# Three-layer attention and MoE chain in fp32 parts: the last two layers in token blocks of 512, 512, 512 and 256

## The chip, the cores and the metric

The kernel runs on one core of a Trainium2 chip. The metric is the device time of one execution in microseconds (us). The profile is of one execution of its own; its times are counted from the first instruction.

## What is computed

Attention with a sigmoid in place of the softmax (4 sequences, 12 heads, 448 tokens, head size 64), a layer that takes the maximum of three products and multiplies by an output matrix, and a layer with a gated unit of width 2048. All tensors are fp32.

```python
scores = q @ k.T / sqrt(64) - log(448)
x = (sigmoid(scores) @ v)                       # 1792 tokens x 768
h = maximum(maximum(x @ w1, x @ w2), x @ w3)    # layer one, 768 wide
y = h @ w_out                                   # layer two
h = y @ w_in                                    # layer three, 2048 wide
g = h * sigmoid(1.702 * h)
out = g @ w_out2                                # layer four
```

## The kernel before

TensorE multiplies in a type (fp32r) that keeps only the upper part of an fp32 number, so every operand is split into an upper and a lower part, and a product is three matmuls into the same PSUM bank: upper weights by upper data, upper weights by lower data, lower weights by upper data (lines 374 to 376, and 608 to 610). Weights are tiles of 128 by 128; the moving operand is 448 tokens wide, one sequence. Each matmul has its own weight load, also where two matmuls in a row use the same weights.

Stages. First, pairs of heads: scores (lines 424 and 426), sigmoid, and the product with the values (line 461, or line 453 in plain fp32 for six of the 24 pairs), in "beats" between which layers one and two of finished sequences are placed (`unit1`, `unit2`). Layer two writes its result, split in its parts (`yst`), to DRAM (`yk`, line 570), six tiles a sequence. Then layers three and four: the 2048 columns are taken in eight groups of two tiles of 128. For each group the four weight tiles are read and split (`weights2`), and for each of the four sequences `unit3` makes two tiles of layer three (6 input tiles x 3 matmuls each), passes each through a sigmoid (ScalarE), a product with it, and a split (VectorE, ScalarE), and `unit4` multiplies the two by the six output tiles (2 x 3 matmuls each) and adds each result to an accumulator in SBUF (`acc`, VectorE; in the first group a copy). `unit3` of the next block is written ahead of `unit4` of the present one. In the last group the accumulators go to DRAM; the last one is added and sent in two halves.

PSUM: layer three has two banks (`mms`), layer four six (`pos`). SBUF is allocated in two phases: the pools `late` and `acc` take over the space of the attention stage and of layers one and two when their last operation is done (`to_late`, `to_acc`). The inputs of layer three (`z`) are read back from DRAM once and stay; those of the first sequence (`z0s`) lie in `late`, the others (`zs`) in `acc`, so their reads wait for the end of layer two.

Order. All operations are first collected in an `Order`, with costs such as `MM` for a matmul and due times that follow from TensorE's order. `run` then lists them per engine by a simulated clock and writes the program out in that order; what an engine executes is fixed before the run, and each engine takes its instructions one after the other. A cast (`copy`) may go to ScalarE or VectorE, as the planner chooses.

Addresses. A weight tile begins at word 48 of its buffer (`OFF`), its data at word 0 (all sizes are multiples of 64 words). In the attention stage the keys, which are the weights there, begin at word 464 (`KEYS`), so 16 beyond a multiple of 64. The outputs of the gate, the moving operand of layer four, begin at the word given by `G_OFF` for their group: 0, 8, 16, 24, 32, 40, 4, 60.

## Time and profile before

| | us |
|---|---|
| median of 3 runs | 987.09 (986.69 to 987.25) |
| the profiled execution | 987.43 |
| its span, first to last instruction | 985.6 |
| TensorE busy in the span | 972.6 |
| VectorE busy | 621.8 |
| ScalarE busy | 347.5 |

Busy time of TensorE is a union of matmuls that overlap, so two matmuls that follow each other are told apart by their starts. PE in a row is TensorE's matmuls, PEld its weight loads, DVE is VectorE, ACT ScalarE, SP the queue that issues DMAs. A number after "L" is the line of the kernel; L225, L222 and L212 are the helpers `two` and `rest`, `copy` and `dma`, so there the tile names tell more.

### The profile page before, as it was taken

Reading aid. Unit: us, or ns where it says so; the run is one execution under the profiler, and the core shown is the slowest. Engines: PE = TensorE matmul, PEld = TensorE weight load, DVE = VectorE, ACT = ScalarE, POOL = GpSimd, SP = SyncE. Lnnn points to the kernel's source line nnn. Section 1 sums busy time; section 2 is a strip of 40 time slices with the busy share of each in tenths; the row PEclk is TensorE's granted clock in tenths of the full one; section 3 lists DMA queues with packets and bytes.
Section 4 is the critical chain, followed back from the end, with each engine's and each line's share of the span. In section 5 each row is a group of like instructions: output and inputs, shape, how many; then the busy total and the mean of one; then the engine's idle time right before and its main releaser. Section 6 shows DMA issues by size and latency. Waiting matters only on the chain.

```text
span 985.6 us, 12195 instructions
## 1 busy us (share of the span) xinstructions
PE 972.6 (99%) x4918; PEld 871.3 (88%) x4918; DVE 621.8 (63%) x945; ACT 347.5 (35%) x514; POOL 1.1 (0%) x6
## 2 busy tenths in 40 slices
PE   8899999999999999999999999999999999999998
PEld 5568888888888889999998999999999999999997
DVE  7989999997577747511112454776757576754344
ACT  6666666953454532111012441221222122121110
POOL 0000000000000000000000000000000000000000
PEclk9999999999999999999999999999999999999999
DMA  7856787996565659996668021110201111000023
GB/s 255 309 189 246 257 307 271 366 380 223 186 206 181 219 178 413 334 348 208 220 217 342 15 80 49 65 65 10 94 26 65 65 65 65 1 1 1 1 103 122
DMA packets 39656, 166.14 MB, mean 169 GB/s; under 512 B 4400, under 2 KB 10288, under 8 KB 39600
## 3 DMA queue, kind: packets, MB, share of 16 engines
q1 hardware_dynamic: 39600, 165.36, 46.7%
q8 instruction: 39, 0.64, 0.3%
q14 instruction: 17, 0.14, 0.0%
HBM read 129.96 MB, written 35.39 MB: 168 GB/s over the span
## 4 chain that ended last, share of the span: by engine, by line
PE 95%; DVE 2%; DMA 1%; issue 0%; SPq 0%; ACT 0%; DVEq 0%
PE mm L374 20%; PE mm L376 19%; PE mm L375 19%; PE po L608 8%; PE po L609 8%; PE po L610 8%; PE sc L424 4%; PE av L461 4%; PE av L453 3%; PE sc L426 1%; DMA raw<-in_wa 1%; PE av L465 1%; DMA v<-in_v 1%; DVE al L225 0%; DVE y L347 0%
## 5 line engine op out<-in xcount | busy, mean ns | idle before, releaser
L374 PE MATMUL mm<-x,w 128*128 128x448 f32 x432 | 159.5, 369 | 0.0
L376 PE MATMUL mm<-x,w 128*128 128x448 f32 x432 | 156.9, 363 | 0.0
L375 PE MATMUL mm<-x,w 128*128 128x448 f32 x432 | 156.6, 363 | 0.0
L225 DVE TENSOR_TENSOR acc<-po,acc 128x448 f32<-128x448 f32 (+1 forms) x169 | 103.8, 620 | 62.9 <-PE po L610 61.6
L608 PE MATMUL po<-g,w 128*128 128x448 f32 x384 | 140.2, 365 | 0.0
L374 PE MATMUL mm<-z,w 128*128 128x448 f32 x384 | 138.9, 362 | 1.2 <-DVE gf L225 1.2
L609 PE MATMUL po<-g,w 128*128 128x448 f32 x384 | 140.1, 365 | 0.0
L610 PE MATMUL po<-g,w 128*128 128x448 f32 x384 | 140.0, 365 | 0.0
L375 PE MATMUL mm<-z,w 128*128 128x448 f32 x384 | 139.4, 363 | 0.0
L376 PE MATMUL mm<-z,w 128*128 128x448 f32 x384 | 138.9, 362 | 0.0
L592 ACT ACTIVATE sg<-mm 128x448 f32<-128x448 f32 x64 | 34.9, 546 | 246.5 <-PE mm L376 246.5
L434 ACT ACTIVATE a<-sc,bias 128x896 f32<-128x896 f32 (+1 forms) x96 | 85.2, 915 | 54.4 <-PE sc L424 42.8
L225 DVE TENSOR_TENSOR gf<-mm,sg 128x448 f32<-128x448 f32 x64 | 39.9, 623 | 84.0 <-ACT sg L592 83.9
L374 PEld LDWEIGHTS mm<-x,w 128*128 128x128 f32 x432 | 80.9, 187 | 13.0 <-issue 7.3
L375 PEld LDWEIGHTS mm<-x,w 128*128 128x128 f32 x432 | 81.1, 188 | 6.3 <-issue 0.6
L376 PEld LDWEIGHTS mm<-x,w 128*128 128x128 f32 x432 | 81.1, 188 | 4.8
L225 DVE TENSOR_TENSOR mx<-mm,mx 128x448 f32<-128x448 f32 x48 | 30.0, 624 | 83.6 <-PE mm L376 83.2
L374 PEld LDWEIGHTS mm<-z,w 128*128 128x128 f32 x384 | 72.0, 187 | 7.0 <-issue 1.6
L610 PEld LDWEIGHTS po<-g,w 128*128 128x128 f32 x384 | 72.1, 188 | 5.8
L608 PEld LDWEIGHTS po<-g,w 128*128 128x128 f32 x384 | 72.0, 188 | 5.8
L609 PEld LDWEIGHTS po<-g,w 128*128 128x128 f32 x384 | 72.1, 188 | 5.7
L375 PEld LDWEIGHTS mm<-z,w 128*128 128x128 f32 x384 | 72.1, 188 | 5.1
(77 smaller groups left out, 1396.9 us busy)
## 6 DMA issues: line engine op xcount, KB each, us to landing
w<-kept SPq DMA_DIRECT2D x72, 768.0 KB, 5.0
raw<-in_wb SPq DMA_DIRECT2D x32, 768.0 KB, 5.3
raw<-in_wa SPq DMA_DIRECT2D x24, 768.0 KB, 4.4
kept<-w SPq DMA_DIRECT2D x24, 768.0 KB, 4.1
t<-in_qk SPq DMA_DIRECT2D x23, 488.0 KB, 4.3
yk<-yst SPq DMA_DIRECT2D x24, 448.0 KB, 5.5
z<-yk SPq DMA_DIRECT2D x24, 448.0 KB, 8.3
out_t<-acc SPq DMA_DIRECT2D x23, 224.0 KB, 1.9
```

The costliest lines, as they stand in the source:

```text
L225: return on("DVE", t_two(n), lambda: dve.tensor_tensor(to(), a(), b(), op=op), [a, b], [to])
L374: pe.matmul(ps(), wh[:, c], xh, start=k == 0, stop=False)
L375: pe.matmul(ps(), wh[:, c], lo(), start=False, stop=False)
L376: pe.matmul(ps(), wl[:, c], xh, start=False, stop=k == KC - 1)
L424: pe.matmul(o[:, e, :], kx[r, keys], qx[r, :S], **how)
L434: on("ACT", t_act(n) + 0.07, lambda: act.activation(a(), ps(), AF.Sigmoid, bias=bias, scale=scale), [ps], [a])
L453: pe.matmul(o, w, x[:, e, :] if c < 3 else x, start=c + e == 0, stop=c == 3)
L461: pe.matmul(av[e](), w, x()[:, e, :], start=c + n == 0, stop=False)
L592: on("ACT", t_act(S), lambda sg=sg, ps=ps: act.activation(sg(), ps(), AF.Sigmoid, scale=1.702), [ps], [sg])
L608: pe.matmul(ps(), wh[:, c], gh, start=j == 0, stop=False)
L609: pe.matmul(ps(), wh[:, c], gl, start=False, stop=False)
L610: pe.matmul(ps(), wl[:, c], gh, start=False, stop=j == 1)
```

## The change

Layers three and four take the 1792 tokens in blocks of 512, 512, 512 and 256 (`TB`) and no longer by sequence. `NB` is still four, so groups, units and their order stay.

For a block of 512 each product is three matmuls as before, with 512 columns. For the block of 256 the upper and lower part lie next to each other, and one matmul of 512 columns passes both through the upper weights: the first 256 columns of the bank get upper by upper, the others upper by lower. A second matmul of 256 columns adds lower weights by upper data to the first half (`terms`). The two halves are then summed: in layer three by a cast of the lower half and an addition ahead of the sigmoid, in layer four by two additions into the accumulator (in the first group a copy and an addition).

Layer two's tiles are cut where a block ends within a sequence, so a tile of sequences two to four is written by two DMAs (`unit2`). The last output is no longer cut in two halves.

The gate's outputs begin at word 0 of their buffer in every group, and the keys at word 496, so 48 beyond a multiple of 64; the tiles of the queries and keys keep their size of 1024 words, but 1008 words and not 976 are loaded and split.

```diff
@@ -21,11 +21,13 @@
 NF = DFF // P
 NPAIR = H // 2
 NP = B * NPAIR
-KEYS = S + 16
+KEYS = S + 48
 QK = KEYS + 3 * P + P
...
 OFF = 48
-G_OFF = (0, 8, 16, 24, 32, 40, 4, 60)
+
+TB = [(0, 512), (512, 512), (1024, 512), (1536, 256)]
+NB = len(TB)
...
-MM = 0.201
+MM, MM512 = 0.201, 0.214
...
-            ("t", [P, QK + 48], 2),
-            ("qh", [P, QK + 48], 2, F32R),
-            ("ql", [P, QK + 48], 2, F32R),
+            ("t", [P, QK + 16], 2),
+            ("qh", [P, QK + 16], 2, F32R),
+            ("ql", [P, QK + 16], 2, F32R),
...
-    z0s = [ring(late, f"z{k}", [P, 2, S], 1, F32R) for k in range(KC)]
-    zs = [ring(acc, f"z{k}", [P, 2, S], B - 1, F32R) for k in range(KC)]
-    gs = ring(late, "g", [P, 4 * S + 64], 2, F32R)
-    sgs = ring(late, "sg", [P, S], 2)
-    gfs = ring(late, "gf", [P, S], 2)
-    accs = ring(acc, "acc", [P, S], B * KC)
+    z0s = [ring(late, f"z{k}", [P, 2, 512], 1, F32R) for k in range(KC)]
+    zs = [ring(acc, f"z{k}", [P, 2, 512], NB - 2, F32R) for k in range(KC)]
+    zrs = [ring(acc, f"zr{k}", [P, 2, 256], 1, F32R) for k in range(KC)]
+    gs = ring(late, "g", [P, 4 * 512], 2, F32R)
+    sgs = ring(late, "sg", [P, 512], 2)
+    gfs = ring(late, "gf", [P, 512], 2)
+    accs = ring(acc, "acc", [P, 512], (NB - 1) * KC)
+    accrs = ring(acc, "accr", [P, 256], KC)
...
-    ykept = [[dram(f"yk{b}_{k}", [P, 2, S]) for k in range(KC)] for b in range(B)]
+    ykept = [[dram(f"yk{t}_{k}", [P, 2, n]) for k in range(KC)] for t, (_, n) in enumerate(TB)]
...
-    def product(ps, w, x):
+    def terms(ps, w, c, x, whole, start, stop):
+
+        wh, wl, xh = w[0]()[:, c], w[1]()[:, c], x[0]()
+        if whole is None:
+            pe.matmul(ps, wh, xh, start=start, stop=False)
+            pe.matmul(ps, wh, x[1](), start=False, stop=False)
+            pe.matmul(ps, wl, xh, start=False, stop=stop)
+        else:
+            pe.matmul(ps, wh, whole(), start=start, stop=False)
+            pe.matmul(ps[:, :256], wl, xh, start=False, stop=stop)
+
+    def product(ps, w, x, mm=3 * MM, whole=None):
         for k, (hi, lo) in enumerate(x):
             c = slice(k * P, (k + 1) * P)
 
-            def f(_, k=k, c=c, hi=hi, lo=lo):
-                wh, wl, xh = w[0](), w[1](), hi()
-                pe.matmul(ps(), wh[:, c], xh, start=k == 0, stop=False)
-                pe.matmul(ps(), wh[:, c], lo(), start=False, stop=False)
-                pe.matmul(ps(), wl[:, c], xh, start=False, stop=k == KC - 1)
-
-            O.pe(f, 3 * MM, [*w, hi, lo], [ps])
+            def f(_, k=k, c=c, x=(hi, lo)):
+                terms(ps(), w, c, x, whole[k] if whole else None, k == 0, k == KC - 1)
+
+            O.pe(f, mm, [*w, hi, lo], [ps])
...
-        dma(ykept[b][m], t, 448, [hi, lo], [ykept[b][m]])
+        for i, (at, n) in enumerate(TB):
+            c0, c1 = max(b * S, at), min((b + 1) * S, at + n)
+            if c0 < c1:
+                to = Part(ykept[i][m].tile, lambda a, s=slice(c0 - at, c1 - at): a[:, :, s])
+                of = Part(t, lambda a, s=slice(c0 - b * S, c1 - b * S): a[:, :, s])
+                dma(to, of, c1 - c0, [hi, lo], [])
+                ykept[i][m].writers.append(O.ops[-1])
...
+    def wide(r, n):
+        return r.tile().part(lambda a: a[:, :n])
+
     def unit3(u):
-        grp, b = divmod(u, B)
+        grp, b = divmod(u, NB)
+        n = TB[b][1]
+        both = n == 256
         if b == 0:
             W[grp] = [weights2(4 * grp + j) for j in range(4)]
         if grp == 0:
-            Z[b] = []
+            Z[b] = [], []
             for k in range(KC):
-                hi, lo, t = split((zs if b else z0s)[k])
-                dma(t, ykept[b][k], 448, [ykept[b][k]], [hi, lo])
-                Z[b].append((hi, lo))
+                hi, lo, t = split((z0s if b == 0 else zrs if both else zs)[k])
+                dma(t, ykept[b][k], n, [ykept[b][k]], [hi, lo])
+                Z[b][0].append((hi, lo))
+                Z[b][1].append(Part(t, lambda a: a.rearrange("p t n -> p (t n)")))
         t = gs.tile()
         gates[u] = []
         for j in range(2):
-            ps = bank(mms)
-            product(ps, W[grp][j], Z[b])
-            sg, gf = sgs.tile().part(), gfs.tile().part()
-            on("ACT", t_act(S), lambda sg=sg, ps=ps: act.activation(sg(), ps(), AF.Sigmoid, scale=1.702), [ps], [sg])
-            two(gf, ps, sg, ALU.mult, S)
-            hi, lo = (t.part(lambda a, j=2 * j + n: a[:, G_OFF[grp] + j * S :][:, :S]) for n in (0, 1))
-            copy(hi, gf, S)
-            rest(lo, gf, hi, S)
-            gates[u].append((hi, lo))
+            ps = wide(mms, 512)
+            product(ps, W[grp][j], Z[b][0], MM512 + MM if both else 3 * MM512, Z[b][1] if both else None)
+            sg, gf = wide(sgs, n), wide(gfs, n)
+            h = ps
+            if both:
+                h = wide(sgs, n)
+                upper, lower = (Part(ps.tile, lambda a, i=i: a[:, i * n :][:, :n]) for i in (0, 1))
+                upper.writers = lower.writers = ps.writers
+                copy(gf, lower, n, psum=True)
+                two(h, upper, gf, ALU.add, n)
+            on("ACT", t_act(n), lambda sg=sg, h=h: act.activation(sg(), h(), AF.Sigmoid, scale=1.702), [h], [sg])
+            two(gf, h, sg, ALU.mult, n)
+            hi, lo = (t.part(lambda a, i=2 * j + i: a[:, i * n :][:, :n]) for i in (0, 1))
+            copy(hi, gf, n)
+            rest(lo, gf, hi, n)
+            gates[u].append((hi, lo, Part(t, lambda a, j=j: a[:, 2 * j * n :][:, : 2 * n])))
 
     def unit4(u):
-        grp, b = divmod(u, B)
+        grp, b = divmod(u, NB)
+        at, n = TB[b]
+        both = n == 256
         g, w = gates.pop(u), W[grp][2:]
         for o in range(KC):
-            ps, c = bank(pos), slice(o * P, (o + 1) * P)
+            ps, c = wide(pos, 512), slice(o * P, (o + 1) * P)
 
             def f(_, ps=ps, c=c):
                 for j in range(2):
-                    wh, wl, gh, gl = w[j][0](), w[j][1](), g[j][0](), g[j][1]()
-                    pe.matmul(ps(), wh[:, c], gh, start=j == 0, stop=False)
-                    pe.matmul(ps(), wh[:, c], gl, start=False, stop=False)
-                    pe.matmul(ps(), wl[:, c], gh, start=False, stop=j == 1)
-
-            O.pe(f, 6 * MM, [y for z in (*w, *g) for y in z], [ps])
+                    terms(ps(), w[j], c, g[j], g[j][2] if both else None, j == 0, j == 1)
+
+            O.pe(f, 2 * (MM512 + MM) if both else 6 * MM512, [y for z in w for y in z] + [y for z in g for y in z[:2]], [ps])
+            parts = [ps]
+            if both:
+                parts = [Part(ps.tile, lambda a, i=i: a[:, i * n :][:, :n]) for i in (0, 1)]
+                for x in parts:
+                    x.writers = ps.writers
             if grp == 0:
-                ACC[b, o] = accs.tile().part()
-                copy(ACC[b, o], ps, S, psum=True)
-                continue
+                a = ACC[b, o] = wide(accrs if both else accs, n)
+                copy(a, parts.pop(0), n, psum=True)
             a = ACC[b, o]
-            cuts = [slice(0, S)] if u < NG * B - 1 or o < KC - 1 else [slice(0, S // 2), slice(S // 2, S)]
-            for h in cuts:
-                pa, aa = (Part(x.tile, lambda t, x=x, h=h: (x.cut(t) if x.cut else t)[:, h]) for x in (ps, a))
-                pa.writers, aa.writers = ps.writers, a.writers
-                two(aa, pa, aa, ALU.add, h.stop - h.start) if len(cuts) > 1 else two(a, ps, a, ALU.add, S)
-                if grp == NG - 1:
-                    src = aa if len(cuts) > 1 else a
-                    O.op(
-                        {"SP": (h.stop - h.start) / 2 / 330.0},
-                        lambda e, src=src, h=h, o=o: sp.dma_start(out[o, :, b * S : (b + 1) * S][:, h], src()),
-                        [src],
-                        [],
-                    )
+            for x in parts:
+                two(a, x, a, ALU.add, n)
+            if grp == NG - 1:
+                O.op(
+                    {"SP": n / 2 / 330.0},
+                    lambda e, a=a, o=o: sp.dma_start(out[o, :, at : at + n], a()),
+                    [a],
+                    [],
+                )
...
+    for u in range(NG * NB):
+        if u + 1 < NG * NB:
             unit3(u + 1)
         unit4(u)
     first_ops = {o for r in (*xs, w1s, *hs, mxs, yst) for t in r.tiles for o in t.ops}
     gate = O.op({"-": 0.0}, to_acc, after=first_ops)
-    for r in (accs, *zs):
+    for r in (accs, accrs, *zs, *zrs):
         r.gate = gate
```

## Rows read from the trace of the kernel before

**Rows 1.** The page: busy time by engine, and the chain that ended last.

```profile
PE 972.6 (99%) x4918; PEld 871.3 (88%) x4918; DVE 621.8 (63%) x945; ACT 347.5 (35%) x514; POOL 1.1 (0%) x6
...
PE 95%; DVE 2%; DMA 1%; issue 0%; SPq 0%; ACT 0%; DVEq 0%
```

**Rows 2.** Stretches: length, busy (count) of PE, PEld, DVE, ACT, POOL; clock, DMA.

```profile
0.00:245.00 245.00, 236.94 (x1211) 192.15 (x1212) 222.21 (x318) 159.55 (x217) 1.08 (x6) 1.00 0.77 280
...
515.20:981.90 466.70, 465.44 (x2309) 432.53 (x2307) 270.59 (x433) 106.59 (x176) 0.00 (x0) 1.00 0.18 65
```

**Rows 3.** Timeline of PE: start, length, instruction; between the layers, and the last matmul.

```profile
515.26 0.36 PE L374 MATMUL mm<-z,w 128*128 128x448 f32 x1
...
515.86 0.36 PE L374 MATMUL mm<-h,w 128*128 128x448 f32 x1
...
522.86 0.37 PE L376 MATMUL mm<-z,w 128*128 128x448 f32 x1
524.48 0.44 PE L374 MATMUL mm<-z,w 128*128 128x448 f32 x1 [1.25 <-DVE gf L225]
...
981.52 0.37 PE L610 MATMUL po<-g,w 128*128 128x448 f32 x1
```

**Rows 4.** Timeline of all engines in the last group: a matmul, load and next matmul.

```profile
958.49 0.37 PE L610 MATMUL po<-g,w 128*128 128x448 f32 x1
958.50 0.19 PEld L374 LDWEIGHTS mm<-z,w 128*128 128x128 f32 x1
958.70 0.36 PE L374 MATMUL mm<-z,w 128*128 128x448 f32 x1
```

**Rows 5.** Line 453: timeline of its loads, and its instructions (ns, min/median/max).

```profile
60.33 0.19 PEld L453 LDWEIGHTS av<-a,v 128*128 128x128 f32 x1 [0.19 <-issue]
...
63.34 0.19 PEld L453 LDWEIGHTS av<-a,v 128*128 128x128 f32 x1 [0.18 <-issue]
...
L453 PEld LDWEIGHTS av<-a,v x84: 186/190/191, 8.6 to 156.5; 128*128 128x128 f32 x84
```

**Rows 6.** Warming matmuls: the timeline, and line 637's instructions (ns, min/median/max).

```profile
1.66 4.10 PE L637 MATMUL av<-yst 128*128 128x448 f32 x10 [1.66 <-POOL yst L296]
...
L637 PEld LDWEIGHTS av<-yst x10: 285/330/333, 1.7 to 4.8; 128*128 128x128 f32 x10
L637 PE MATMUL av<-yst x10: 575/575/739, 1.7 to 5.2; 128*128 128x448 f32 x10
```

**Rows 7.** Stretches, instructions on `po` alone (PE, PEld, DVE, ACT): groups 0, 1.

```profile
546.10:560.50 14.40, 7.52 (x36) 6.75 (x37) 0.00 (x0) 3.20 (x6) 1.00 0.00 1
...
589.40:603.90 14.50, 7.67 (x36) 6.68 (x36) 3.68 (x6) 0.00 (x0) 1.00 0.33 110
```

**Rows 8.** Second group (589.4 to 647.5): stretch, VectorE's groups of instructions; last: the tail.

```profile
589.40:647.50 58.10, 58.10 (x288) 53.79 (x287) 38.82 (x63) 13.37 (x21) 0.00 (x0) 1.00 0.16 55
...
L225 DVE TENSOR_TENSOR acc<-po,acc 128x448 f32<-128x448 f32 x24 | 14.8, 626 | 8.0 <-PE po L610 7.7
L225 DVE TENSOR_TENSOR gf<-mm,sg 128x448 f32<-128x448 f32 x8 | 5.0, 622 | 6.8 <-ACT sg L592 6.8
L225 DVE TENSOR_TENSOR g<-gf,g 128x448 fp32r<-128x448 f32 x7 | 4.4, 634 | 1.3 <-ACT g L222 1.3
...
L225 DVE TENSOR_TENSOR acc<-po,acc 128x224 f32<-128x224 f32 x2 | 0.7, 386 | 0.6 <-PE po L610 0.6
...
981.92 0.69 DVE L225 TENSOR_TENSOR acc<-po,acc 128x224 f32<-128x224 f32 x2 [0.60 <-PE po L610]
```

**Rows 9.** Between the layers: the chain of waits (start, us), and SP's timeline.

```profile
523.26 0.55 ACT sg L592
523.84 0.64 DVE gf L225
...
520.65 14.59 SPq L212 DMA_DIRECT2D z<-yk  x18
```

**Rows 10.** First 245 us: VectorE's remainders of queries and keys, by shape.

```profile
L225 DVE TENSOR_TENSOR ql<-t,qh 128x976 fp32r<-128x976 f32 x18 | 21.1, 1170 | 0.0
...
L225 DVE TENSOR_TENSOR ql<-t,qh 128x464 fp32r<-128x464 f32 x1 | 0.6, 643 | 0.0
```

More of the change, by code (lines that the diff above doesn't have):

```diff
@@ L656, in moe_chain_kernel @@
     unit3(0)
-    for u in range(NG * B):
-        if u + 1 < NG * B:
+    for u in range(NG * NB):
+        if u + 1 < NG * NB:
             unit3(u + 1)
```

## The prediction

> **What bounds the kernel now.** The first view is the page's busy line and its chain of waits [rows 1]: TensorE is busy for 99% of the span and stands for 95% of the chain, so only what changes the spacing of its matmuls, or makes it wait, moves the time. The second is the table by stage [rows 2]. In layers three and four (515.2 to 981.9 us) TensorE is busy for 465.44 of 466.70 us, and VectorE for 270.59. So in these layers I count matmuls and multiply by their spacing. The durations in the rows (0.36 us) are no use for that, since they overlap; starts are.
>
> From the first matmul of layer three at 515.26 to the last of layer four at 981.52 are 466.26 us [rows 3]. Three matmuls of layer two lie between (from 515.86, 0.60 us) and one stall (522.86 to 524.48, 1.42 us longer than a plain spacing). What is left, 464.2 us, is 2303 spacings, a mean of 201.6 ns; all 2304 make 464.4 us.
>
> What sets 201.6 ns? At the granted clock of 1.00 [rows 2], the 2.4 GHz level, 448 columns are 448/2.4 = 186.7 ns, so about 15 ns are unexplained. The rows of single instructions [rows 4] show the order: the load of a matmul's weights starts with the matmul before it (958.50), takes 0.19 us, and the matmul follows at 958.70. Load plus handover is 200 ns, longer than the columns. I read this as: spacing = the larger of load path (200) and columns. Two other rows test it. The plain f32 products of line 453 stream their columns twice (84 records for 42 calls): eight spacings from 60.33 to 63.34 are 376 ns each, 2.7 ns above 896/2.4 = 373.3, with a load of 190 ns inside [rows 5]. And the ten warming matmuls at the start, of the same type and shape as those of layer three, took (4.10 - 0.575 - 0.164)/9 = 373 ns each, with loads of 330 ns [rows 6]; both are longer there than later, but the gap between load and spacing is 43 ns and not 13. So where columns outlast the load, the load is hidden whole.
>
> **The change, part by part.**
>
> *Wide blocks.* There are 192 weight tiles (16 by 6 in each of the two layers). Each now meets three blocks of 512 columns with three matmuls, plus one 512-column matmul in the narrow block, 10 in all: 1920 matmuls. By the reading above each costs its columns, 512/2.4 = 213.3 ns, and a little more. No row has a 512-column matmul. The lower end is 213.3; the upper end, if the 2.7 ns of line 453 is per matmul, is 216.0. If those 2.7 ns are shared by its two passes, 214.7. I take 215: 1920 x 0.215 = 412.8 us; the ends give 409.5 and 414.7.
>
> *The narrow block's second matmul.* 192 matmuls have 256 columns, 106.7 ns. The next load can't be in before its 187 to 190 ns are over, so the spacing is that of the load path. In the trace that path depends on the operands' offset: layer four's 36 matmuls of a unit keep TensorE busy for 7.52 us in group 0, whose offset is 0, and 7.67 us in group 1, whose offset is 8 [rows 7]; less two tails of 0.16 us that is 200.0 and 204.2 ns. All offsets are now 0, so I take 200.5: 192 x 0.2005 = 38.5 us. The ends: 109 ns, 106.7 and the 2.7 of line 453, if the load doesn't bind (20.9 us), 206 ns if the relief of the offset fails (39.6 us).
>
> The rows' load is 187 to 190 ns [rows 4, 5]. The Trainium skill ("TensorE: Matmul & The Clock Gate", section on LDWEIGHTS) puts a load at its columns over 1.2, so 107 ns for 128; by it the 256-column matmul would cost about 109 ns and the sum would be 17.6 us lower. The trace's duration is what I use, and the rule becomes a rival.
>
> The same page (section "Wait — 56ns, not 53.3ns?") gives a full-clock spacing of columns over 2.4 plus about 2.5 ns. By that a wide matmul would be 215.8 ns and the sum 1.5 us higher than mine; no row here has 512 columns.
>
> Sum of layers three and four: 412.8 + 38.5 = 451.3 against 464.4 us, a gain of 13.1 us. The offset itself gives nothing in the wide blocks, where the load path of up to 206 ns lies under 213 ns.
>
> *VectorE.* In one group of 58.1 us it is busy for 38.82 us; 24 additions into the accumulators, 8 products with the gate and 7 remainders take 24.2 us, so the new weights cost about 14.6 us [rows 8]. From 386 ns at 224 and 626 at 448 columns, 256 columns cost 420 ns and 512 some 695. Per group now: 30 instructions of 512 (18 + 6 + 6) make 20.9 us; the narrow block adds 12 accumulations, 2 copies, 2 sums, 2 products and 2 remainders, 20 x 0.42 = 8.4 us; with weights 43.9 us of about 56.4. It stays under TensorE's time. In the narrow stretch alone it is 8.4 us against 9.96 us of TensorE (24 x 0.415). What hides the longer chain (copy, sum, sigmoid, product, copy, remainder: six steps, about 2.8 us) is layer four of the block before, 36 x 0.215 = 7.7 us, which stands between the narrow block's layer three and layer four; and the PSUM bank is free again after the second step. Cost taken: nothing. If the cover is gone, each narrow unit costs up to 2.8 us, 8 of them 22 us.
>
> *Between the layers.* The stall at 524.48 is TensorE's last product, sigmoid (0.55) and multiplication (0.64) until its bank is free [rows 9]; at 512 columns both are about 0.07 longer, +0.1 us. The loads of z wait in SP's queue for the last write of y and begin at 520.65, 18 in 14.59 us. Now the last y tile leaves in two DMAs, so one more issue (0.32 us) stands ahead of them. SP then has 12 more issues in the stage before, behind which only loads of kept weights queue. Blocks of 512 need 512 KB a tile, 8/7 of the time, but six matmuls for each tile also take 1.29 instead of 1.20 us. Taken: +0.1; bounds 0 and +1.
>
> *Tail.* The last output was added in two halves (0.69 us, [rows 8]); now there are two additions of 256 and one DMA: 0.04 to 0.15 us more. Taken 0.1.
>
> *Attention stage.* The keys move by 32 columns, so 25 casts and remainders are longer: 643 ns at 464 and 1170 at 976 columns [rows 10] make 33 ns each, 0.8 us of VectorE, 1.1 with the casts on it. VectorE is busy for 222 of 245 us there [rows 2], so between 0 and all of it is on the path. Against it, the scores take the offset that products have: at most the 4.2 ns of [rows 7] on 288 spacings, 1.2 us. I take 0, bounds -1.2 and +1.1.
>
> Total: the profiled execution took 987.43 us (span 985.6). 987.4 - 13.1 + 0.1 + 0.1 = 974.5 us. The median of the runs is 0.34 lower, so **974.2 us**, 1.3% faster.
>
> **The rivals.**
>
> 1. *The handover comes on top of the columns.* Then a wide matmul costs 213.3 + 13.6 = 226.9 ns, layers three and four 435.6 + 38.5 = 474.1, and the kernel takes 997 us, slower. It decides from 221.8 ns a matmul, (464.4 - 38.5)/1920. For it: each f32r matmul at full clock has those 13 to 15 ns. Against it: [rows 5, 6], where the gap is 2.7 ns and none. Chance 0.04.
>
> 2. *The load is shorter than its row.* The 256-column matmul then runs at 109 ns: 956.6 us. For it: 187 is just what 448 columns take, so the row could hold a wait. Against it: the same 186 to 191 ns inside matmuls twice as long [rows 5]. Chance 0.04. (The Trainium skill's rule on LDWEIGHTS, above, is of this kind.)
>
> 3. *VectorE comes late around the narrow block.* Its order is fixed ahead by the planner; weights for the next group (14.6 us a group) may be queued before the narrow sums. Two weight tiles ahead (7.3 us) plus the chain of 2.8 exceed the cover of 7.7 by 2.4 us; in two to four of the seven groups that is 5 to 10 us, 979 to 984 us. Against it: 12 us a group stay free. Chance 0.07.
>
> 4. *The attention stage is planned anew and waits more.* The longer casts change the planner's order. TensorE idles for 8 us in the first 245 [rows 2]; half as much again gives 978 us. Chance 0.06.
>
> **How the numbers follow.** My forecast holds 0.79, with 970.5 to 977 as its own range (409.5 to 414.7 for the wide part, the ends of the attention stage, the narrow offset). The range of 970 to 980 us takes in rival 4 and the start of rival 3; outside lie rivals 1, 2 and most of 3. A difference under 0.2%, 2 us, can't be told from none here. Faster by more: 0.79 + 0.04 + 0.06 and nearly all of rival 3, 0.94; the same 0.02; slower 0.04.
>
> **What would show it.** Starts of successive wide matmuls 214 to 216 ns apart; at 225 rival 1 holds. A 256-column matmul followed 200 ns later by the next; at 110 rival 2. TensorE's records fall by 192 to about 4726. No idle time of TensorE with VectorE as the releaser around the narrow blocks; if there is, rival 3. The first matmul of layer three at 515 +/- 1 us; if later, rival 4.

## The result, and the profile after

The changed kernel takes 993.4 us (median of 20 runs, 987.0 to 999.0) against 987.6 us (986.3 to 990.1) for the kernel before on the same chip: a ratio of 1.0054, 95% interval 1.0039 to 1.0069. It is slower by half a per cent where 1.3% faster was forecast, and its runs are spread over 12 us, not 4. Its profiled execution took 989.05 us, one of its faster ones; its span is 987.3 us against 985.6.

The busy line and the chain of the page, to be held against [rows 1]:

```profile
PE 972.6 (99%) x4726; PEld 822.4 (83%) x4726; DVE 637.3 (65%) x1001; ACT 361.3 (37%) x537; POOL 1.1 (0%) x6
...
PE 90%; DVE 4%; DMA 3%; issue 1%; ACT 1%; SPq 0%; DVEq 0%
```

TensorE has 192 matmuls fewer, as planned, and is busy for the same 972.6 us: what the count saved, the single matmul gave back. VectorE, ScalarE and DMA appear in the chain with 8% where they had 3%: new waits.

The stretches show where (columns as in [rows 2]; the cuts are at the first matmul of layer three and after the last of layer four):

```profile
0.00:245.00 245.00, 235.66 (x1201) 190.35 (x1202) 219.59 (x313) 162.22 (x219) 1.08 (x6) 1.00 0.77 280
245.00:518.10 273.10, 272.30 (x1411) 248.23 (x1410) 130.42 (x196) 81.61 (x121) 0.00 (x0) 1.00 0.70 248
518.10:983.30 465.20, 464.61 (x2116) 383.79 (x2114) 286.24 (x491) 117.46 (x197) 0.00 (x0) 1.00 0.18 64
```

Layer three begins at 518.1 us and not at 515.3: 2.8 us lost ahead of the part that was rewritten. From its first matmul to the last of layer four are 464.8 us instead of 466.3: 1.4 us won, where 13 were forecast.

The timeline of TensorE around the narrow block's matmuls in layer four (start, length, instruction; PEld is a load):

```profile
581.63 0.39 PE L380 MATMUL po<-g,w 128*128 128x512 f32 x1
581.64 0.19 PEld L381 LDWEIGHTS po<-g,w 128*128 128x128 f32 x1
...
581.86 0.28 PE L381 MATMUL po<-g,w 128*128 128x256 f32 x1
581.86 0.19 PEld L380 LDWEIGHTS po<-g,w 128*128 128x128 f32 x1
581.98 0.40 PE L380 MATMUL po<-g,w 128*128 128x512 f32 x1
```

The 512-column matmul is followed after 0.23 us and the 256-column one after 0.12. The second number says that [rows 4] was misread: the load that begins at 581.86 is recorded until 582.05, but the matmul that uses it starts at 581.98. The recorded length of a load is not what the next matmul waits for.

Nine wide matmuls of layer four in a row, the first and the last two; eight spacings, 1.83/8 = 229 ns:

```profile
710.17 0.39 PE L377 MATMUL po<-g,w 128*128 128x512 f32 x1
...
711.77 0.39 PE L378 MATMUL po<-g,w 128*128 128x512 f32 x1
712.00 0.39 PE L376 MATMUL po<-g,w 128*128 128x512 f32 x1
```

The waits of TensorE over the whole execution (total us, times, longest):

```profile
PE av L465 <- DVE xf L499: 4.5, 2, 2.6
...
PE mm L376 <- ACT w L224: 1.0, 1, 1.0
PE mm L376 <- DMA w<-kept: 0.8, 1, 0.8
PE mm L376 <- DMA z<-yk: 0.5, 1, 0.5
PE mm L378 <- DVE w L227: 0.3, 1, 0.3
```

The waits for `w` are in the attention stage, at 193.5, 194.5 and 381.8 us; before, TensorE had none of them. No wait is near a narrow block.

### The profile page after: what moved, and what is told of

It reads as the page before. It is cut to its first block, busy times and chain, and to the rows that moved or that the text cites. A ratio compares the mean times of both kernels' runs of the same rounds, so it can differ in the third digit from the quotient of the medians.

```text
span 987.3 us, 11962 instructions
## 1 busy us (share of the span) xinstructions
PE 972.6 (99%) x4726; PEld 822.4 (83%) x4726; DVE 637.3 (65%) x1001; ACT 361.3 (37%) x537; POOL 1.1 (0%) x6
## 4 chain that ended last, share of the span: by engine, by line
PE 90%; DVE 4%; DMA 3%; issue 1%; ACT 1%; SPq 0%; DVEq 0%
PE mm L376 18%; PE mm L378 17%; PE mm L377 17%; PE po L378 7%; PE po L376 7%; PE po L377 7%; PE av L473 4%; PE sc L436 4%; PE mm L380 2%; PE av L465 2%; PE po L380 2%; DMA raw<-in_wa 2%; PE mm L381 1%; PE po L381 1%; PE sc L438 1%; DMA w<-kept 1%
## 5 line engine op out<-in xcount | busy, mean ns | idle before, releaser
L376 PE MATMUL mm<-z,w 128*128 128x512 f32 x288 | 113.1, 393 | 0.5 <-DMA z<-yk 0.5
L227 DVE TENSOR_TENSOR acc<-po,acc 128x512 f32<-128x512 f32 x126 | 87.0, 691 | 40.9 <-PE po L378 40.5
L378 PE MATMUL mm<-z,w 128*128 128x512 f32 x288 | 113.1, 393 | 0.0
L378 PE MATMUL po<-g,w 128*128 128x512 f32 x288 | 113.1, 393 | 0.0
L376 PE MATMUL po<-g,w 128*128 128x512 f32 x288 | 113.0, 392 | 0.0
L377 PE MATMUL mm<-z,w 128*128 128x512 f32 x288 | 112.3, 390 | 0.0
L377 PE MATMUL po<-g,w 128*128 128x512 f32 x288 | 112.1, 389 | 0.0
L623 ACT ACTIVATE sg<-mm 128x512 f32<-128x512 f32 x48 | 28.7, 599 | 182.9 <-PE mm L378 182.8
L227 DVE TENSOR_TENSOR gf<-mm,sg 128x512 f32<-128x512 f32 x48 | 33.2, 691 | 96.3 <-ACT sg L623 96.3
L227 DVE TENSOR_TENSOR al<-a,ah 128x896 fp32r<-128x896 f32 x72 | 68.6, 969 | 0.2
L338 ACT ACTIVATE y<-raw 128x768 f32<-128x768 f32 x56 | 50.9, 913 | 40.8 <-DVE w L227 16.9
L376 PEld LDWEIGHTS mm<-z,w 128*128 128x128 f32 x288 | 54.1, 188 | 12.5 <-issue 0.9
L378 PEld LDWEIGHTS po<-g,w 128*128 128x128 f32 x288 | 54.1, 188 | 12.1
L378 PEld LDWEIGHTS mm<-z,w 128*128 128x128 f32 x288 | 54.1, 188 | 12.0
```

What stands on the lines that cost most here:

```text
L227: return on("DVE", t_two(n), lambda: dve.tensor_tensor(to(), a(), b(), op=op), [a, b], [to])
L338: on("ACT", t_act(DM), lambda: act.activation(y(), words(raw(), F32, 1), AF.Copy, scale=2.0**-112), [raw], [y])
L376: pe.matmul(ps, wh, xh, start=start, stop=False)
L377: pe.matmul(ps, wh, x[1](), start=False, stop=False)
L378: pe.matmul(ps, wl, xh, start=False, stop=stop)
L623: on("ACT", t_act(n), lambda sg=sg, h=h: act.activation(sg(), h(), AF.Sigmoid, scale=1.702), [h], [sg])
```

## The experiments

Two questions: what sets the spacing of a matmul, and what happened ahead of layer three. Times beside "before" are of the kernel before on the same chip in the same hours.

**The old keys in the changed kernel.**

```diff
-KEYS = S + 48
+KEYS = S + 16
-            ("t", [P, QK + 16], 2),
+            ("t", [P, QK + 48], 2),
```

(the same for `qh` and `ql`)

> The changed kernel with the keys back at word 464 and 976 words loaded and split; blocks, split writes and the gate's offset 0 as changed. In the changed kernel layer three begins at 518.1 us and not 515.3, and its runs lie between 987 and 999 us. Theory K (the longer casts made the planner order the attention stage anew, and the new order waits): layer three begins at 515.3 +/- 0.5, the kernel takes 986 +/- 1 us (987.1 less the 1.4 us that layers three and four gained, 466.5 to 465.1) and its runs lie within 4 us. Rival W (layer two's split writes, 42 DMAs and not 24, hold up SP's queue and the kept weights behind them): layer three begins at 517 or later, median 990 or more, runs spread over 8 us or more.

Median 987.5 us (12 runs, 985.4 to 993.4), ratio 1.0006, interval 0.9989 to 1.0022: the same as before. In its profile layer three begins at 515.2 us and the waits at 193 to 195 us are gone; the one for kept weights stays (0.6 us at 379). The traces show the planner's part too: with the old keys TensorE, VectorE and ScalarE run the attention stage in the very order of the kernel before, with the new keys the orders part at 20 to 23 us. So theory K holds for the late start. But this profile was of an execution of 992.2 us, and its loss sat elsewhere, in layers three and four: 470.5 us. Theory K's narrow spread did not come.

**The new keys in the kernel before.**

```diff
-KEYS = S + 16
+KEYS = S + 48
-            ("t", [P, QK + 48], 2),
+            ("t", [P, QK + 16], 2),
```

> The kernel before with the keys at word 496 and 1008 words loaded and split; nothing else. Theory K: layer three begins later than 515.3 by 1 to 5 us and the median is 989 to 995 us, with a spread of 8 us or more. Rival W: 987 +/- 1 us with a spread of 4 us. If the offset of the keys were worth something by itself, the scores' spacing of 202.5 ns falls to 200 and stage one gains up to 0.7 us.

Median 990.9 us (989.3 to 994.1), ratio 1.0033, interval 1.0021 to 1.0045. Layer three begins at 518.1 us, and layers three and four take the 466.5 us of before. The keys alone, with no new blocks, cost 3 us (with one stretch of granted clock 0.5 at 31 us, of which more below). The order of the attention stage parts from that of the kernel before at the same place as in the changed kernel. Theory K's spread of 8 us or more did not come: it is 4.8 us. What the offset gives the scores is not seen beside it.

**One offset for the gate in the kernel before.**

```diff
-G_OFF = (0, 8, 16, 24, 32, 40, 4, 60)
+G_OFF = (0,) * 8
```

> The kernel before with the gate's outputs at offset 0 in all groups (448 columns, three matmuls). Theory: the operands' offset sets part of the gap between columns and spacing. Layer four's spacing falls from 202.8 ns to 200.1 ns, 1152 x 2.7 = 3.1 us, so 984.2 us. Rival: the groups differ for another reason (later groups share the time with VectorE's work on new weights); then the later groups stay at 203 to 205 ns and the time at 987.3.

Median 983.9 us (983.1 to 984.2), ratio 0.9958, interval 0.9946 to 0.997. All eight groups of layer four now have a mean spacing of 200.0 ns (single spacings 197 to 202), and layers three and four take 462.7 us. The offset is the cause of the differences between groups, and the kernel with this one line is faster than either. It also divides the gain of the changed kernel: of 466.3 - 464.8 us the offset alone is worth 3.6, so the blocks lost 2.1 in this profile.

**Whole writes of layer two.** Layer two's tiles are written by sequence again; layer three's are read in pieces.

```diff
-            c0, c1 = max(b * S, at), min((b + 1) * S, at + n)
-            if c0 < c1:
-                ...
+        dma(ykept[b][m], t, 448, [hi, lo], [ykept[b][m]])
```

> The changed kernel, but layer two writes each tile with one DMA as before (by sequence) and layer three's tiles are read in one or two pieces where a block lies over two sequences (42 reads and not 24). Theory K: stage one keeps its late start of layer three (517 or later) and its spread; median 990 to 996. Rival W: layer three begins at 515.5 +/- 1, the spread falls to 4 us, median 986 to 988 (the stall between the layers may grow by up to 2 us, since the second pieces are issued late).

Median 1002.4 us (1001.5 to 1006.9), ratio 1.0156. Layer three begins at 520.5 us and the wait for kept weights at 384 us is still there, so the split writes are not the cause of either: rival W falls. The edit has a cost of its own, which was underrated: the second pieces are ordered after the first, and TensorE waits 7.9 us for them, until 547.7 us; layers three and four take 476.4 us. From 542.4 to 552.6 us the granted clock is 0.50, the 1.2 GHz level, and there the wide matmuls start 427 ns apart:

```profile
548.29 0.63 PE L377 MATMUL mm<-z,w 128*128 128x512 f32 x1
548.72 0.63 PE L378 MATMUL mm<-z,w 128*128 128x512 f32 x1
549.14 0.63 PE L376 MATMUL mm<-z,w 128*128 128x512 f32 x1
```

427 ns is 512/1.2 and nothing more: at this level the same matmul, with a load of its own, loses nothing.

**A second profile of the changed kernel, and three more.** The kernel is unaltered.

> The changed kernel, unaltered, for a second profile: its runs lie between 987 and 999 us, the first profile was one of 989 us. If this one is slower, the stage in which it is slower tells where the spread is from. Stage one varies (theory): layer three begins between 516 and 527 us, and the time from there to the end stays at 469 +/- 0.5 us. Rival: the matmuls' spacing varies from run to run; then the time of layers three and four differs by more than 1 us.

> The changed kernel, unaltered, for a third profile (the first two, of 989.1 and 991.5 us, had layers three and four at 464.8 us). Theory M: a run over 994 us has its wide matmuls at the level of 233.3 ns from the second group on, so 470.5 us for layers three and four, beside a late stage one. Rival: such a run has the lower level, and all its excess in stage one (layer three begins at 523 us or later, with two or more stretches of granted clock 0.5 in the first 100 us).

> The same for a fourth profile: layer three begins at 518.1 us without a stretch of granted clock 0.5 in the first 100 us, and 2 to 3 us later for each such stretch of 3.4 us; layers three and four take 464.8 or 470.5 us and nothing between.

> The same for a fifth profile, with the same two theories: theory M puts what is over 992 us in layers three and four, its rival in stage one.

These executions took 991.5, 993.7, 990.6 and 991.8 us. Layers three and four took 464.8 us in every one, to 0.03 us. All the difference is in the attention stage: layer three begins at 520.6, 522.8, 519.6 and 520.9 us. The windows of the longest of the four show what is behind it (length; busy of PE, PEld, DVE, ACT, POOL; granted clock; DMA):

```profile
0.00:245.00 245.00, 233.99 (x1177) 186.62 (x1178) 214.55 (x306) 158.82 (x215) 1.08 (x6) 0.98 0.77 276
...
28.80:35.60 6.80, 6.01 (x8) 2.52 (x8) 6.74 (x10) 3.35 (x5) 0.00 (x0) 0.50 0.77 263
62.90:66.30 3.40, 3.31 (x5) 1.65 (x6) 1.82 (x4) 1.03 (x2) 0.00 (x0) 0.50 0.88 283
...
522.80:988.00 465.20, 464.62 (x2116) 383.72 (x2114) 286.18 (x491) 117.62 (x197) 0.00 (x0) 1.00 0.18 64
```

A granted clock of 0.50 is the 1.2 GHz level. Ahead of it TensorE stood idle. First this execution's timeline, then that of the first profile, which had the same wait and kept its clock:

```profile
26.65 0.36 PE L438 MATMUL sc<-qh,ql 128*128 128x448 f32 x1
29.59 6.25 PE L465 MATMUL av<-a,v 128*128 128x448 f32 x8 [2.58 <-DVE xf L499]
```

```profile
26.59 0.36 PE L438 MATMUL sc<-qh,ql 128*128 128x448 f32 x1
29.55 3.27 PE L465 MATMUL av<-a,v 128*128 128x448 f32 x8 [2.59 <-DVE xf L499]
```

In the kernel before, and in the changed kernel with the old keys, the same wait for VectorE's `xf` is 1.7 us:

```profile
28.81 3.27 PE L453 MATMUL av<-a,v 128*128 128x448 f32 x8 [1.71 <-DVE xf L487]
28.86 3.27 PE L465 MATMUL av<-a,v 128*128 128x448 f32 x8 [1.68 <-DVE xf L499]
```

The new order of the casts makes it 2.6, and in most executions TensorE's clock falls within or after it: eight matmuls take 6.25 us instead of 3.27. Over all the profiles of this document the wait is 2.6 us in the ten with the new keys, and the clock fell in eight of them, between 28.8 and 31.0 us; it is 1.7 us in the seven with the old keys, and the clock fell in none. One such stretch of 3.4 us goes with a start of layer three at 519.6 to 520.9 (the two later ones also wait 1.6 to 1.7 us for kept weights, the earliest 0.5), the 6.8 and 3.4 us of this execution with 522.8, none with 518.1. So in these five profiles the difference is stage one's, as theory M's rival has it. But none of the four executions was over 994 us, where theory M speaks, so it was not tested here; the run times given with the old keys' profiles below bear on it.

**Widths.** Four of an output tile's six matmuls get fewer columns, in every second group fewer weights too.

```diff
+                    n = (512, 448, 384, 320, 256, 128)[o]
+                    m = 64 if grp % 2 else 128
...
+                    pe.matmul(ps()[:m, :n], wh[:, :m], gl[:, :n], start=False, stop=False)
```

> Layer four of the three wide blocks leaves out part of its work: of the six matmuls of an output tile the first and the last have 512 columns, and the four between have 512, 448, 384, 320, 256 and 128 columns for output tiles 0 to 5; in every second group those four also use only 64 of the 128 columns of the weights. The changed kernel gave 229.5 ns at 512, 118.5 at 256, the one before 200.0 at 448 with offset 0. Theory C (the load's reads slow the stream, a fixed loss per load): with 128 weight columns the spacing is columns/2.4 plus 13 to 16 ns at every width above 256, so 175 at 384 and 148 at 320, and at 128 columns the load binds (110 to 120 ns or more); with 64 weight columns the loss is halved, 6 to 8 ns (194 at 448). Theory H (a fixed handover whatever is loaded): the same with 128 weight columns, and no change with 64. Theory S (the stream itself runs slower): spacing is 8 + 0.433 x columns, 174.4 at 384, 146.7 at 320, and no change with 64 weight columns. The forecast's reading (the larger of 200 and columns) gives 200 at all widths up to 448.

Mean spacing of two successive matmuls of the same form, from the starts, and what is left after columns/2.4:

| columns | 128 weight columns, ns | left | 64 weight columns, ns | left |
|---|---|---|---|---|
| 512 | 230.4 | 17.1 | 228.5 | 15.2 |
| 448 | 200.0 | 13.3 | 203.2 | 16.5 |
| 384 | 173.1 | 13.1 | 171.9 | 11.9 |
| 320 | 146.1 | 12.7 | 144.7 | 11.3 |
| 256 | 117.8 | 11.1 | 116.6 | 9.9 |
| 128 | 93.3 (58 to 113) | - | 59.9 | 6.6 |

The timeline of the group with 320 and 128 columns shows the last row's two values:

```profile
542.12 0.31 PE L652 MATMUL po<-g,w 128*128 128x320 f32 x1
542.26 0.31 PE L649 MATMUL po<-g,w 128*128 128x320 f32 x1
...
543.96 0.22 PE L650 MATMUL po<-g,w 128*128 128x128 f32 x1
544.02 0.27 PE L652 MATMUL po<-g,w 128*128 128x128 f32 x1
544.13 0.28 PE L649 MATMUL po<-g,w 128*128 128x128 f32 x1
544.24 0.28 PE L650 MATMUL po<-g,w 128*128 128x128 f32 x1
```

What is left grows with the columns, from 7 ns at 128 to 15 to 17 at 512, and hardly changes when the load is halved (at 448 columns it is 3 ns higher). With 64 weight columns the whole range is (228.5 - 59.9)/384 = 0.439 ns a column plus 4 ns. Theories C and H fall (C wants the loss halved with 64 weight columns; H wants one loss at every width, where 15 to 17 ns were measured at 512, 10 to 11 at 256 and, with 64 weight columns, 6.6 at 128), as does the forecast's reading, which would have 200 ns down to 128 columns. Theory S stands: the data stream itself runs some 5% slower than 1/2.4 ns a column. Only at 128 columns does the load bind, 110 ns from 544.02 on. The groups of load rows (busy us and mean ns after the first bar) say how 110 goes with a row of 188:

```profile
L650 PEld LDWEIGHTS po<-g,w 128*128 128x128 f32 x144 | 27.1, 188 | 3.6
L650 PEld LDWEIGHTS po<-g,w 128*64 128x64 f32 x144 | 19.4, 134 | 5.5
```

64 weight columns are 54 ns, so of the 188 ns some 108 go by columns and some 80 don't hold up the next matmul (an estimate from these two rows). The Trainium skill ("TensorE: Matmul & The Clock Gate", section on LDWEIGHTS) puts a load at its columns over 1.2, which makes 107 ns here, and the trace agrees with it, not with the 188 ns of the load's row.

**The gate's offsets at 512 columns.**

```diff
-            hi, lo = (t.part(lambda a, i=2 * j + i: a[:, i * n :][:, :n]) for i in (0, 1))
+            hi, lo = (t.part(lambda a, i=2 * j + i: a[:, G_OFF[grp] + i * n :][:, :n]) for i in (0, 1))
```

> The changed kernel with the gate's outputs at the offsets of the kernel before (0, 8, 16, 24, 32, 40, 4, 60 words by group). Theory C (load and stream meet at the memory): the spacing of 512 columns depends on the offset as that of 448 did, 229.5 at 0 and 232 to 235 at 8, 32 and 40. Theory H: 229.5 +/- 0.5 in all groups.

Means of layer four's wide matmuls by group: 229.3 at offset 0; 233.3, 232.1, 233.7, 233.1, 233.0, 231.6, 231.2 at 8, 16, 24, 32, 40, 4, 60. Layers three and four took 467.6 us instead of 464.8. So the loss depends on the offset at 512 columns too: the forecast's sentence that the offset gives nothing in the wide blocks was wrong. This is what theory C expected; with the widths it says that the place of the data, not the size of the load, counts. The values lie near the higher of the two levels shown below, but the offset does not just choose the level: layer three's wide matmuls, whose data stay at offset 0, keep to means of 228.9 to 229.4 ns in six of groups two to eight (230.6 in the other), while at the higher level they too are at 233.

**Three matmuls in the narrow block.** No operand of both parts, and no sums of halves.

```diff
+        if whole:
+            ps, whole = ps[:, :256], None
```

> The narrow block with three matmuls of 256 columns for each weight tile, and no sums of halves; wide blocks as changed. If every matmul costs columns/2.4 plus a loss of 12 to 16 ns, the narrow block costs 192 x 3 x 119 = 68.5 us and not 192 x (232 + 119) = 67.4, so 1.1 us more, less VectorE's and ScalarE's sums, which nobody waits for: the same within 0.2% as the changed kernel, apart from its stage one. By the forecast's reading it would be 192 x 3 x 200 = 115 us, 48 us more.

In its profile layers three and four took 465.2 us instead of 464.8, and the 256-column matmuls were 117.8 ns apart. There passing both parts through the upper weights is worth 0.4 us, and the extra work on VectorE that it needs costs nothing that could be seen. The runs say something else: 988.9 us median (984.0 to 992.8), ratio 1.0003, interval 0.9989 to 1.0018, the same as before, where the changed kernel has 1.0054 (1.0039 to 1.0069), each against the kernel before on its own chip. So this kernel is some half a per cent faster than the changed one, though TensorE, VectorE and ScalarE run the attention stage in the same order, and "the same within 0.2%" did not come. The profile is of the longest of the ten runs (granted clock 0.50 for 10.2 us, layer three begun at 522.3 us), so it doesn't hold the gain; the next section says what is likely.

**Two more profiles with the old keys.** Unaltered.

> The changed kernel with the old keys, unaltered, for a second profile. Its first profile was one of 992.2 us, and there the wide matmuls of groups two to eight were 233.0 to 233.3 ns apart in the mean and not 229.0 as in the first group and in the changed kernel's profiles; layers three and four took 470.5 us and not 464.8. Theory M (a wide matmul's spacing settles at one of two levels from run to run): the time from layer three's first matmul to layer four's last is 464.8 if the run takes 985 to 987 us, and up to 5.7 us more, by the units at the higher level, if it takes more. Rival: the spread is from stage one; then a time over 988 us goes with a start of layer three later than 517 us.

> The same kernel for a third profile, with the same two theories: by theory M each of its units lies at a mean of 229.0 to 229.3 or of 233 ns in its wide matmuls, and the run's time over 985.5 us is 1728 x 4 ns by the share of units at the higher level.

The second took 987.7 us: layers three and four at 464.8, wide matmuls at a mean of 229.1, layer three begun at 516.4. The third took 991.3 us: 470.5 us, 233.2 ns, begun at 514.4. In the first and the third the wide matmuls changed their level once, behind the first narrow block's layer four (at 584 and 583 us), and stayed to the end. In the narrow block the 512-column matmuls go the other way: 232 to 233 ns at the lower level, 230 at the higher. The timeline of the first at the place shown above, again nine matmuls, 1.87/8 = 234 ns:

```profile
709.27 0.40 PE L378 MATMUL po<-g,w 128*128 128x512 f32 x1
...
710.90 0.40 PE L376 MATMUL po<-g,w 128*128 128x512 f32 x1
711.14 0.40 PE L377 MATMUL po<-g,w 128*128 128x512 f32 x1
```

Theory M holds for this kernel: two levels, nothing between, 5.7 us apart over the two layers, with the granted clock at 1.00 in both. What chooses the level is not shown.

The run times say that the changed kernel has both levels too, though its five profiles all had the lower one. A stretch of 3.4 us at half the clock lowers the mean granted clock of an execution of 990 us by 0.0017. At each mean granted clock its 20 runs fall into two bunches:

| mean granted clock | lower bunch, us | upper bunch, us |
|---|---|---|
| 0.999 and 1.000 | 986.99, 989.05, 989.18, 989.52 | 993.42, 994.11, 994.53, 995.25 |
| 0.998 | 988.22, 990.12, 990.29, 991.30 | 995.58, 996.99, 997.07 |
| 0.995 and 0.996 | 992.14, 993.34, 993.91 | 998.93, 999.03 |

Down the table the clock takes its part; across it the means of the bunches lie 5.6 to 6.6 us apart, about the 5.7 us between the levels, and the clock can't be the reason in the first row, where it takes about 1 us at most. The 12 runs with the old keys fall apart in the same way (eight from 985.4 to 989.1 us, four from 991.4 to 993.4), and there profiles show the level. So the higher level is the likely reason for nine of the 20 runs; none of them has a trace, so it is not shown. With three matmuls in the narrow block none of the ten runs lies in the upper bunch, so the narrow block's operand of both parts may bring the higher level; that is not shown either.

**bf16 in the same place.** Output tiles 1, 3 and 5 of the wide blocks get four matmuls of zeros in bf16 in the middle.

```diff
+                        pe.matmul(y, nought[:, 576:704], x, start=False, stop=False)
```

> The changed kernel with the old keys; layer four of the wide blocks leaves out part of its work: for output tiles 1, 3 and 5 the four middle matmuls of six are of zeros in bf16, weights and data (512 columns, for tile 3 256 columns). Theory S (the stream of the fp32r type is what runs slower, 0.43 to 0.44 ns a column): bf16 matmuls of 512 columns follow each other in 213.3 to 216 ns, those of 256 in 107 to 110. Rival H (every matmul with a load of its own has a handover of 11 to 17 ns): 229 and 118 ns as for fp32r.

The timeline with 512 and with 256 columns:

```profile
591.91 0.10 PEld L653 LDWEIGHTS <-nought 128*128 128x128 bf16 x1
592.13 0.38 PE L653 MATMUL po<-nought 128*128 128x512 bf16 x1
592.13 0.10 PEld L655 LDWEIGHTS <-nought 128*128 128x128 bf16 x1
592.34 0.38 PE L655 MATMUL po<-nought 128*128 128x512 bf16 x1
592.56 0.38 PE L656 MATMUL po<-nought 128*128 128x512 bf16 x1
...
594.74 0.27 PE L653 MATMUL po<-nought 128*128 128x256 bf16 x1
594.85 0.27 PE L655 MATMUL po<-nought 128*128 128x256 bf16 x1
```

Medians of 216 and 109 ns: 213.3 and 106.7 plus 2.5. (The first spacing of each four is longer, 227 and 120 ns.) At the same width the fp32r stream takes 229, so rival H falls: each of these matmuls has a load of its own (all of the same tile) and loses 2.5 ns. The Trainium skill's full-clock spacing (the same page, section "Wait — 56ns, not 53.3ns?"), columns over 2.4 plus 2.5 ns, holds for bf16 here and not for fp32r. One reservation: the load of a bf16 tile is shorter as well, 0.10 us in its row and not 0.19, so this run alone would not part the stream from the load; the widths do.

**Other offsets in the kernel before.**

```diff
-G_OFF = (0, 8, 16, 24, 32, 40, 4, 60)
+G_OFF = (12, 20, 28, 36, 44, 48, 52, 56)
```

> The kernel before with eight other offsets of the gate's outputs (12, 20, 28, 36, 44, 48, 52, 56 words by group). The eight of before gave means of 200.0 to 205.2 ns at 448 columns (0: 200.0, 24: 200.9, 16 and 60: 203, 8: 205). Theory C2 (the loss in the stream depends on where data and weights, which begin at word 48, lie to each other): the means differ from group to group by 1 to 5 ns and repeat within a group; 48, where both begin alike, is the worst. If the stream's loss had a floor whatever the offset, no group falls under 199.5 ns.

Means by group: 206.6, 205.8, 204.2, 203.9, 202.6, 202.7, 200.1, 206.6 ns; 990.0 us. They differ by up to 6.6 ns, and 48, where data and weights begin alike, is not the worst. None is under 200.0. Of the sixteen offsets tried, 0 and 52 are best; the law behind them is not found.

## Why the prediction was wrong, point by point

*What bounds the kernel.* Right: TensorE is the bound before and after, and its spacing decides.

*The spacing.* This is the step that failed. "The larger of the load path (200) and columns" fitted one width only, since every matmul of the trace had 448 columns. 448 columns at the fp32r pace are 200 ns, and load plus handover happened to be recorded as 200 too. The wide matmul was sized at 215 ns and measured 229.5: (464.9 - 0.6 of layer two - 0.8 of stalls - 22.9)/1920. That is 440.6 instead of 412.8 us, 27.8 more. The 256-column matmul was sized at 200.5 and measured 119.1: 22.9 instead of 38.5 us, 15.6 less. Together the two layers' matmuls take 463.5 us where 451.3 were forecast and 464.4 were spent before.

Both spacing rivals thus came at once, near their numbers (226.9 ns of rival 1 for 229.5, 109 of rival 2 for 119), and the second gave back over half of what the first cost. By their own numbers both together would have made 435.6 + 20.9 = 456.5 us; 463.5 were measured, since each matmul was some 3 and 10 ns dearer still. Rival 1's mechanism is not right: the loss is no fixed handover, since it shrinks with the columns. The two tests that made it unlikely read rows of another pace. The 376 ns of line 453, in plain fp32, are of one record of 448 columns, and a call has two records; whether a record passes its columns twice or at half the pace the rows don't tell. The warming matmuls of [rows 6] took 373 ns, which is 448/1.2, the pace of the 1.2 GHz level; the trace holds no granted clock before 6.8 us, so the 1.00 of [rows 2] doesn't speak for them. At 1.2 GHz nothing is lost, as the 427 ns for 512 columns in the run with whole writes show. [Rows 7] pointed the right way: the spacing moved by 4 ns with the place of the data, which a bound set by the load doesn't explain.

*The offset.* Read rightly at 448 columns (200.0 ns with offset 0 in all groups, 202.8 before); that wide blocks hide it was wrong.

*VectorE and the narrow chain.* Right: no wait of TensorE lies near a narrow block, and rival 3 did not come.

*Between the layers.* Stalls of 0.8 us in place of 1.4: 0.6 less, where 0.1 more was taken with bounds of 0 and +1.

*The attention stage.* Sized at nothing, bounds -1.2 and +1.1, but 2.8 us in the first profile and up to 7.5 in the others. The arithmetic of longer casts was not the price. The price was the planner's order, which changed at 20 us and after (rival 4, chance 0.06). It cost 2.8 us in the first profile, of which 2.1 are idle time of TensorE (9.3 us instead of 8.1 in the first 245 us, 0.8 instead of none after). Of the waits, 0.8 us are for kept weights, whose cause is open (0.6, 0.3 us and none in the three profiles with the old keys). The wait of 2.6 us at 27 us was followed by a fall of the clock in four of five.

*Sum.* For the first profile: 987.43 - 1.45 + 2.85, and 0.2 at the end, make 989.0 us; 989.05 was measured. The median lies 4.3 us above it. Part of that is what the clock takes in the attention stage; the rest is, by the run times, most likely the higher level of the wide matmuls, which no trace of the changed kernel shows.

## What to carry to other kernels

A spacing read at one width fits any law, so before blocks are made wider, look for a matmul of the same type and clock with another number of columns; where the time goes by columns, fewer and wider matmuls save next to nothing: at one offset twelve matmuls of 448 cost 2400 ns, and the ten of 512 and one of 256 that took their place 2414. A change of an operand's size far from the rewritten part makes a planner order that part anew, which may cost more than the rewrite wins; change one at a time. Sort run times by their granted clock before one profile is taken for all. Test the cheap part alone: the offset, one line, gave 0.42% (983.9 us) where the whole change lost 0.54%.

## What the runs showed of the hardware

- At the 2.4 GHz level fp32r data stream at about 0.44 ns a column and not 0.417 (128 to 512 columns), bf16 at 0.42 (216 and 109 ns at 512 and 256). At the 1.2 GHz level 512 fp32r columns take 427 ns, 512/1.2, so nothing is lost there. Plain fp32 takes 376 ns for a record of 448 columns, two records a call.
- The loss depends on where the data begin: 200.0 to 206.6 ns for the same 448-column matmul over 16 offsets.
- 512-column fp32r matmuls settle at one of two levels in an execution, means of 229.0 or 233.3 ns, without any change of the granted clock; in three profiles of the kernel with the old keys it was the higher one twice, in five of the changed kernel never, though its run times lie in two bunches about as far apart as the levels.
- A weight load's row is longer (0.19 us) than the time after which its matmul can start (0.12 us after the load's start). The rows are 188 ns at 128 weight columns, 134 at 64, and 98 for 128 columns of bf16.
- After an idle 2.6 us TensorE's granted clock was 0.50 for 3.4 us in three of the changed kernel's five profiles, for 6.8 us in one, and did not fall in one; over all profiles it fell after this wait in eight of ten, and after a wait of 1.7 us in the same place in none of seven.
